# A fused attention and mixer kernel: first query cast shared by two engines, finer pieces of the first keys, earlier pairs of score rounds, and new constants for the static schedule

## The chip, the cores and the metric

The kernel runs on one core of a Trainium2 chip. The metric is the device time of one execution in microseconds (us). An execution counts as fast when it lies within 1.5% of the fastest of its kernel; slow executions are left out of all times and ratios.

## The reference, cut to what matters

```
scores = q @ k^T / sqrt(64) - log(448);  attn = sigmoid(scores);  x = attn @ v
# q, k, v: 8 batches x 12 heads x 448 positions x 64, float32; the heads are put side by side: x is 8 x 448 x 768
h  = relu(x^T @ w_tok1) @ w_tok2          # token mixing, 448 -> 256 -> 448
u  = x + h^T
out = u + relu(u @ w_ch1) @ w_ch2         # channel mixing, 768 -> 1536 -> 768
```

The sigmoid is element by element, so there is no softmax sum to wait for. Heads are handled in quads, three to a batch. A **score round** is four score matmuls, for 64 keys of the four heads of a quad; one sigmoid on ScalarE follows it. (In the very first quad rounds cover half of the heads.)

## The kernel before: the parts that matter here

The program is laid out by a list scheduler in Python that runs before compilation. It keeps an estimated clock for every engine, asks at each step which operations are ready, and takes the one with the best priority. The order it finds is fixed in the program; on the chip the engines only wait for each other. So a changed estimate changes the order of instructions, often far from the place where the estimate was meant to act.

Score rounds have two PSUM slots.

```
for i, hs in both:
    ps = plan.buf("wide", 2, [128, 2, 512], FP32, "psum", f"qk_{b}_{m}_{i}_{hs[0]}")   # two slots
    ...
    nc.tensor.matmul(out=ps[64*s : 64*s+64, h, 0:S], lhsT=kT[...], rhs=qT[...])          # 4 of these
    ...
    nc.scalar.activation(out=at[:, hs, :], in_=ps[:, hs, 0:S], func=SIGMOID, ...)
```

TensorE loses about 0.1 us when it changes between its tiling modes (64-row score and value matmuls, 128-row products); the prediction works this out from the trace. For that reason rounds are grouped in pairs. For batch 1, whose attention is computed beside the mixing of batch 0, the first seven rounds go singly:

```
parts = [[o] for o in rs[:7]] + [rs[i : i + 2] for i in range(7, 21, 2)] + [[o] for o in rs[21:]]
```

The constants REST and REST1 say how much other work (in us of TensorE's time) must be done before the next group of second token products may be taken at its ordinary priority (REST1 is for batch 1; a line left out here gives batch 0's a fixed priority):

```
p = 4.5 if o.name[:2] == "K2" and o.name[-1] == "0" and state["rest"] < (REST1 if o.name[:4] == "K2_1" else REST) else rank
```

The first head's queries come in float32 and are cast by one ScalarE instruction; its transposes on TensorE are cut at position 4, and the second head's keys are kept whole:

```
def cast(raw=raw, h=hs[0]):
    nc.scalar.activation(out=t[:, h, :, :], in_=raw[:, :, :], func=COPYF)
...
whole = [((0, 4), (4, J))]
if lone and hs[0] == 0:
    whole = [((0, 2),), ((2, J),)] if what == "k" else [((0, 4),), ((4, J),)]
```

In the traces, qk is a score matmul, xa a value matmul, c<-uT the first channel product, c<-w_ch the second, kt the first use of the token weights w_tok2, yn and yt second token products, ut a transpose, tq and tk transposes of queries and keys.

## Time and profile before

| kernel before | value | where from |
|---|---|---|
| time | 372.8 us (372.73 to 372.81, 3 runs) | the runs |
| span of the profiled execution | 381.5 us, granted clock 0.949: slow | the cores view |
| span of a second profile of the same kernel | 371.2 us, granted clock 1.0: fast | the cores view |
| TensorE busy in the fast one | 364.5 us of 371.2 (98%) | the page, part 1 |

The prediction had only the slow profile. All comparisons after it use the second, fast profile, which is the first experiment below. "Busy" for TensorE says little here: matmuls overlap and a waiting matmul counts in part. To find lost time I took the start of each matmul, subtracted it from the start of the next, and compared the difference with the streaming time of its columns.

### The profile page before, as it was taken

To read this page: it belongs to the slowest core of one execution; us is meant where nothing else is said; L and a number is where in the kernel's file an instruction comes from. 1 tells how busy PE (TensorE), PEld (TensorE's weight loads), DVE (VectorE), ACT (ScalarE), POOL (GpSimd) and SP (SyncE) were. 2 spreads that over 40 slices of the span, in tenths; PEclk is the share of its full clock that TensorE was granted. 3 is DMA by queue.
4 is the path that set the end of the run, shared out by engine and by line. 5 is a ranking of instruction groups with operands and counts; after the bars stand their busy time and mean duration, and the time that the engine had idled before them with its cause. 6 is when DMAs were issued, how large, how long until landed. Compare 5 with 4: busy or idle time off the path is not lost.

```text
span 381.5 us, 7956 instructions
## 1 busy us (share of the span) xinstructions
PE 374.4 (98%) x3188; PEld 188.2 (49%) x3188; DVE 177.0 (46%) x414; ACT 208.0 (55%) x269; POOL 115.8 (30%) x261
## 2 busy tenths in 40 slices
PE   7999999999999999999999999999999999999995
PEld 4454444554454544455444545544455555555553
DVE  4576345643424545542354335744451358654221
ACT  5997773476677866786667476564556311100000
POOL 8982227144544435334444242350000000000000
PEclk9999999999999999999999999999999999999999
DMA  6999999599989999999998999993004452401344
GB/s 96 185 201 206 210 206 193 107 181 142 142 131 140 196 142 132 124 159 207 166 129 134 182 162 177 184 131 67 18 12 113 101 124 53 63 0 43 82 103 105
DMA packets 97013, 50.06 MB, mean 131 GB/s; under 512 B 70544, under 2 KB 93456, under 8 KB 96976
## 3 DMA queue, kind: packets, MB, share of 16 engines
q0 software_dynamic: 24080, 21.62, 41.7%
q1 hardware_dynamic: 72656, 27.62, 40.2%
q8 instruction: 25, 0.41, 0.4%
q10 hardware_dynamic: 240, 0.31, 0.3%
q14 instruction: 12, 0.10, 0.1%
HBM read 43.45 MB, written 11.01 MB: 143 GB/s over the span
## 4 chain that ended last, share of the span: by engine, by line
PE 94%; POOL 2%; DMA 1%; DVE 1%; ACT 1%; issue 0%; ACTq 0%; POOLq 0%
PE c L1026 30%; PE c L1085 30%; PE qk L595 11%; PE xa L633 9%; PE yn L952 5%; PE k L876 4%; DMA k<-in_k_dram 1%; POOL k L345 1%; PE xb L692 1%; PE k L726 1%; PE k L836 1%; PE k L860 1%; PE tq L540 1%; POOL q L345 1%; PE tk L540 1%; PE yt L910 1%
## 5 line engine op out<-in xcount | busy, mean ns | idle before, releaser
L611 ACT ACTIVATE attn<-qk,att_bias 128x896 f16<-128x896 f32 (+1 forms) x172 | 161.1, 986 | 79.4 <-PE qk L595 76.5
L1026 PE MATMUL c<-uT,w_ch 128*128 128x448 f16 x576 | 122.1, 362 | 0.0
L1085 PE MATMUL c<-w_ch,h2aT 128*128 128x384 f16 x576 | 103.7, 334 | 0.0
L1042 DVE TENSOR_SCALAR h2aT<-c 128x384 f16<-128x384 f32 x96 | 53.5, 557 | 76.6 <-PE c L1026 76.5
L1026 PEld LDWEIGHTS <-w_ch 128*128 128x128 f16 x576 | 54.1, 99 | 60.0 <-issue 12.7
L1085 PEld LDWEIGHTS <-h2aT 128*128 128x128 f16 x576 | 55.7, 100 | 42.6 <-issue 5.8
L1098 DVE TENSOR_TENSOR u<-u,c 128x384 f32<-128x384 f32 x48 | 26.6, 554 | 64.6 <-PE c L1085 64.5
L595 PE MATMUL qk<-qT,kT 64*64 64x448 f16 x672 | 52.6, 366 | 0.6 <-ACT attn L611 0.5
L800 POOL COPY mark<-attn 1x1 f16<-1x1 f16 x54 | 9.6, 178 | 96.6 <-ACT attn L611 96.5
L633 PE MATMUL xa<-attn,v 64*64 64x448 f16 x672 | 37.8, 359 | 0.0
L974 DVE TENSOR_TENSOR u<-x,yn 128x384 f32<-128x384 f16 x48 | 24.7, 550 | 18.0 <-PE yn L952 17.9
L595 PEld LDWEIGHTS <-kT 64*64 64x64 f16 x672 | 14.0, 104 | 31.3 <-issue 29.0
L982 ACT ACTIVATE u<-u 128x768 f16<-128x768 f32 x21 | 17.6, 843 | 19.1 <-DVE u L974 19.1
L670 ACT ACTIVATE xT<-xa 128x448 f16<-128x448 f32 (+2 forms) x61 | 22.1, 439 | 7.5 <-PE xa L633 7.5
L633 PEld LDWEIGHTS <-v 64*64 64x64 f16 x672 | 19.8, 109 | 12.6 <-issue 0.7
L512 POOL COPY qp<-q 128x384 f16<-128x384 f16 (+1 forms) x54 | 21.3, 432 | 11.8 <-DMA q<-in_q_dram 11.0
L512 POOL COPY kp<-k 128x384 f16<-128x384 f16 (+1 forms) x54 | 21.2, 429 | 10.8 <-DMA k<-in_k_dram 10.4
L952 PE MATMUL yn<-h,w_tok 128*128 128x384 f16 x104 | 22.3, 334 | 0.2 <-ACT xT L670 0.2
L1042 DVE TENSOR_SCALAR h2odd<-c 128x64 f16<-128x64 f32 x96 | 20.6, 215 | 0.0
L889 DVE TENSOR_SCALAR h<-k 128x384 f16<-128x384 f32 x24 | 12.8, 557 | 10.2 <-PE k L876 10.2
L1085 PE MATMUL c<-w_ch,h2odd 128*128 128x384 f16 x96 | 17.5, 334 | 0.0
L356 POOL DMA_DIRECT2D q<-in_q_dram x21 | 15.0, 715 | 7.4 <-issue 5.5
(73 smaller groups left out, 208.5 us busy)
## 6 DMA issues: line engine op xcount, KB each, us to landing
out_dram<-u SPq DMA_DIRECT2D x48, 192.0 KB, 2.9
k<-in_k_dram POOLq DMA_DIRECT2D x21, 224.0 KB, 4.7
q<-in_q_dram POOLq DMA_DIRECT2D x21, 224.0 KB, 5.2
v<-in_v_dram POOLq DMA_DIRECT2D x21, 224.0 KB, 5.4
w_ch<-in_moe_w_ch_dram POOLq DMA_DIRECT2D x6, 768.0 KB, 19.1
out_dram<-ut SPq DMA_DIRECT2D x6, 192.0 KB, 3.4
v<-in_v_dram POOLq DMA_DIRECT2D x6, 112.0 KB, 5.2
x<-xT SPq DMA_TRANSPOSE x32, 3.9
```

What stands on the lines that cost most here:

```text
L512: nc.gpsimd.tensor_copy(out=pm[:, to, :, :], in_=src[:, fr, :, :])
L595: nc.tensor.matmul(out=ps[64 * s : 64 * s + 64, h, 0:S], lhsT=kT[64 * h : 64 * h + 64, i, s, :], rhs=qT[64 * h : 64 * h + 64, :, s, :], st ...
L611: nc.scalar.activation(out=at[:, hs, :], in_=ps[:, hs, 0:S], func=SIGMOID, bias=bias_t[:, :], scale=att_scale,)
L633: nc.tensor.matmul(out=ps[s](slice(64 * h, 64 * h + 64)), lhsT=vf[64 * s : 64 * s + 64, h, order[i], :], rhs=attn[i][64 * s : 64 * s + 64, ...
L670: nc.scalar.activation(out=xt[:, s, to : to + n], in_=ps[s](every)[:, fr : fr + n], func=COPYF)
L952: nc.tensor.matmul(out=ps[:, :], lhsT=w_tok2[:, t, s0 : s0 + 2, :], rhs=h1[b][:, t, c], start=(t == 0), stop=(t == 1),)
L974: nc.vector.tensor_tensor(out=to, in0=x, in1=y, op=ADD)
L982: nc.scalar.activation(out=u16[rows, :], in_=utile[rows, :] if blk == 3 else u[b][:, blk, :], func=COPYF)
L1026: nc.tensor.matmul(out=ps[:, :], lhsT=w_ch1[cb // 4][:, db, 128 * (cb % 4) : 128 * (cb % 4) + 128], rhs=uT[b][:, db, :], start=(db == 0), ...
L1042: nc.vector.tensor_scalar(out=to, in0=ps[:, fr], scalar1=0.0, scalar2=None, op0=MAX)
L1085: nc.tensor.matmul(out=ps[:, :], lhsT=h, rhs=w, start=(cb == 0), stop=(cb == NCB - 1))
L1098: nc.vector.tensor_tensor(out=t, in0=t, in1=ps[:, :], op=ADD)
```

## The change

The intent: shorten the first 20 us, in which ScalarE and the loads set the pace, by letting the first score come earlier; then order the stretch where batches 0 and 1 are worked on together so that TensorE has fewer mode changes and waits.

```
-        self.hitch = [(8.6, 1.1), (15.2, 1.4), (19.5, 0.8), (21.9, 0.5)]
+        self.hitch = [(0.1, 0.5), (7.5, 0.3), (8.65, 1.1), (12.4, 0.4), (15.4, 1.0), (19.5, 0.8), (21.9, 0.5)]
...
-    LEAD, SPAN, REST, LATE = 18.0, 0.86, 1.0, 0
+    LEAD, SPAN, REST, LATE = 18.0, 0.86, 1.1, 0
-    JOIN, PULL, ALONE = 0.05, 3.0, 3.5
-    REST1 = 0
-    PAUSE = 1.5
+    JOIN, PULL, ALONE = 0.15, 1.5, 3.5
+    REST1 = 0.1
+    PAUSE = 1.3
...
-                    def cast(raw=raw, h=hs[0]):
-                        nc.scalar.activation(out=t[:, h, :, :], in_=raw[:, :, :], func=COPYF)
+                    for js in (slice(0, 4), slice(4, J)):
+                        eng = "ACT" if not js.start else "DVE"
+                        ...   # ScalarE casts positions 0 to 3, VectorE 4 to 6
...
-            whole = [((0, 4), (4, J))]
+            whole = [((0, 4, 1), (4, J, 1))]
+            if lone and hs[0] and what == "k":
+                whole = [((0, 4, 1),), ((4, J, 1),)]
             if lone and hs[0] == 0:
-                whole = [((0, 2),), ((2, J),)] if what == "k" else [((0, 4),), ((4, J),)]
+                whole = [((0, 2, 1),), ((2, J, 1),)] if what == "k" else [((0, J, 2),), ((1, J, 2),)]
...   # the rest follows from spans having a step; a line that gave the second head's transposes priority is gone
-                parts = [[o] for o in rs[:7]] + [rs[i : i + 2] for i in range(7, 21, 2)] + [[o] for o in rs[21:]]
+                parts = [[o] for o in rs[:5]] + [rs[i : i + 2] for i in range(5, 21, 2)] + [[o] for o in rs[21:]]
```

I call the cast, the transposes and the kept pieces "the start", the last line "the pairs", and REST with REST1 "the rests". "hitch" is a table of expected delays of the loads.

More of the change, by code (lines that the diff above doesn't have):

```diff
@@ L334, in fetch, with cast @@
                             )
-                    def cast(raw=raw, h=hs[0]):
-                        nc.scalar.activation(out=t[:, h, :, :], in_=raw[:, :, :], func=COPYF)
                     o = op("fetch_q", "SQ", 3.0, fetch, uses=[raw])
-                    yield op("cast_q", "ACT", 0.6, cast, [o, warm], [raw, t], rank=-2)
+                    pieces = []
+                    for js in (slice(0, 4), slice(4, J)):
+                        eng = "ACT" if not js.start else "DVE"
+                        def cast(raw=raw, h=hs[0], js=js, eng=eng):
+                            if eng == "ACT":
+                                nc.scalar.activation(out=t[:, h, js, :], in_=raw[:, js, :], func=COPYF)
+                            else:
+                                nc.vector.tensor_copy(out=t[:, h, js, :], in_=raw[:, js, :])
+                        pieces.append(op(f"cast_q{js.start}", eng, 0.09 + 0.075 * (js.stop - js.start), cast, [o, warm], [raw, t], rank=-2))
+                    pieces[0].pieces = pieces
+                    yield pieces[0]
                     continue
@@ L534, in turned, with turn @@
                 parts = []
-                for a, z in spans:
-                    def turn(ps=ps, hs=hs, a=a, z=z):
-                        for i in range(a, z):
+                for a, z, step in spans:
+                    these = range(a, z, step)
+                    def turn(ps=ps, hs=hs, these=these):
+                        for i in these:
                             for h in hs:
@@ L546, in turned @@
                     need = [lds[hs[0]]] if len(lds) > 1 else lds
-                    us = (z - a) * (0.107 if lone and hs[0] == 0 else 0.065)
+                    if step == 2:
+                        need = [need[0].pieces[a]]
+                    us = len(these) * (0.107 if lone and hs[0] == 0 else 0.065)
                     o = op(f"turn{what}_{b}_{m}_{hs[0]}{a}", "PE", us, turn, [*need, ident_op, *hold], [raw, ps, ident, t])
                     o.pri = (0 if what == "q" else 0.05) + (0.35 if m == 2 else 0) if b == 0 else 2.5
-                    if lone and hs[0] and a:
-                        o.pri = -1.5
                     parts.append(o)
@@ L557, in turned @@
                 extra.extend(parts)
-                eng = "ACT" if spans[0] in ((0, 2), (4, J)) else "DVE"
-                pieces = [(eng, slice(spans[0][0], spans[-1][1]))]
+                eng = "ACT" if spans[0] in ((0, 2, 1), (1, J, 2)) else "DVE"
+                pieces = [(eng, slice(spans[0][0], spans[-1][1], spans[0][2]))]
                 for eng, ij in pieces:
@@ L568, in turned @@
                     o = op(
-                        f"keep{what}_{b}_{m}_{hs[0]}{ij.start}", eng, 0.08 + 0.08 * (ij.stop - ij.start), keep, parts, [t, ps], rank=-1 if b == 0 else 0.5
+                        f"keep{what}_{b}_{m}_{hs[0]}{ij.start}", eng, 0.08 + 0.08 * len(range(J)[ij]), keep, parts, [t, ps], rank=-1 if b == 0 else 0.5
                     )
```

## The prediction

> **What bounds the kernel now.** I read the page first, for the busiest engine and for the chain that ended last.
>
> ```profile
> PE 374.4 (98%) x3188; PEld 188.2 (49%) x3188; DVE 177.0 (46%) x414; ACT 208.0 (55%) x269; POOL 115.8 (30%) x261
> ...
> PE 94%; POOL 2%; DMA 1%; DVE 1%; ACT 1%; issue 0%; ACTq 0%; POOLq 0%
> ```
>
> TensorE is busy 98% of the span and carries 94% of the chain; what is not TensorE (POOL, DMA, DVE, ACT, together 5%, some 19 us) lies almost wholly in the first 20 us. The change alters no large piece of TensorE's work, so it can pay only where TensorE waits or changes mode. The profiled execution was a slow one (381.5 us span, granted clock 0.949, against 372.8 us timed). I use it for durations and waits, and apply savings in us to 372.8: waits at the start are mostly other engines' time.
>
> To find TensorE's lost time I compared each matmul's start to the next one's start with its streaming time. In steady runs a 448-column matmul takes 0.197 us from start to start. The chain in order of time shows it, and the price of a mode change:
>
> ```profile
> 36.49 0.68 PE c L1026 x3
> 37.48 0.69 PE c L1026 x3
> 38.49 1.87 PE c L1026 x9
> ```
>
> (1.87 - 0.68) / 6 = 0.198 us a matmul. Between 36.49 and 37.48 there stand three of these (0.59 us) and one score round of 64-row matmuls (one more stream, 0.197 us): 0.99 - 0.79 = 0.20 us is left, two mode changes, about **0.1 us each**. By that account TensorE loses per 2 us about 1.2 us until 10, 0.6 to 0.8 us from 12 to 20, and from 20 us on almost nothing but mode changes, except at two places: near 64 us (0.46 us) and at 105.7 us (0.6 us). So there are three things to look at: the first 20 us, the two bubbles, the count of mode changes.
>
> The timeline shows the start (start, duration, engine, what, idle before and releaser):
>
> ```profile
> 3.79 0.58 ACT L337 ACTIVATE q<-q_first 128x448 f16<-128x448 f32 x1 [0.92 <-DMA q_first<-in_q_dram]
> ...
> 6.14 0.57 PE L595 MATMUL qk<-qT,kT 64*64 64x448 f16 x4
> ...
> 6.56 1.16 ACT L611 ACTIVATE attn<-qk,att_bias 128x448 f16<-128x448 f32 x2 [0.82 <-PE qk L595]
> ...
> 7.96 6.33 ACT L611 ACTIVATE attn<-qk,att_bias 128x448 f16<-128x448 f32 x9 [0.25 <-PE qk L595]
> ...
> 13.79 0.41 PE L540 MATMUL tk<-ident,k 128*64 128x128 f16 x8 [0.16 <-DMA k<-in_k_dram]
> ...
> 14.57 1.01 ACT L611 ACTIVATE attn<-qk,att_bias 128x896 f16<-128x896 f32 x1 [0.28 <-PE qk L595]
> ...
> 15.73 10.76 ACT L611 ACTIVATE attn<-qk,att_bias 128x896 f16<-128x896 f32 x11 [0.15 <-PE qk L595]
> ...
> 16.12 1.16 DVE L664 CAST xT<-xa 128x448 f16<-128x448 f32 x2 [0.64 <-PE xa L633]
> ...
> 21.07 0.95 PE L760 MATMUL kt<-w_tok,h 128*128 128x448 f16 x4
> ...
> 64.64 0.93 PE L952 MATMUL yn<-h,w_tok 128*128 128x384 f16 x4 [0.20 <-ACT xT L670]
> ```
>
> The reader is to see that from 6.56 us the sigmoids on ScalarE nearly touch, with idle times of 0.25, 0.28 and 0.15 us: ScalarE bounds the start, and the 0.28 arises because the score matmul stands behind a transposition that waits for keys landing at 13.65 us. From 16.12 to 20.5 us VectorE works without a break too.
>
> **What the Trainium skill says.** "ScalarE: Activation LUTs", What ACT_TABLE_LOAD costs: an activation with immediate scale and bias takes 186 ns + 0.833 ns per element of the row. For 448 elements that is 559 ns; the trace has 576, so it agrees. "TensorEngine Tiling (Array Packing)", Key Properties: changing the tiling mode drains TensorE; the trace agrees, at 0.1 us a change. "SBUF — State Buffer", SBUF: two separate sides: a VectorE fp32 copy from SBUF to SBUF can take the port pair that GpSimd needs to write DMA descriptors. The kernel before has no such copy, so no run yet shows it; it is a rival below.
>
> **The change, part by part.** The instruction orders of the two programs give the rest.
>
> (a) **The first cast in two.** ScalarE's part falls to 128x256: 0.186 + 0.213 = 0.40 us (estimate by the page), ending near 4.19 instead of 4.37. VectorE's 128x192 is an estimate of 0.25 to 0.35 us, from its copies of 512 and 896 columns (0.417 and 0.627 us, slope 0.55 ns, intercept 0.14 us), ending near 4.1, while VectorE is otherwise idle. Query transposes then go first (odd positions, then even, 0.055 us each, from about 4.25); keys of head 0 landed at 4.46, all seven follow and end near 5.05. ScalarE copies the odd queries (0.48 us, to 5.07), then two keys (0.38 us, to 5.4). The first score matmul no longer stands behind the second head's query transposes, which waited for a landing at 5.75 and start at 5.88 in the timeline. I expect it at 5.43 instead of 6.14, the first sigmoid at 5.85 instead of 6.56: **0.7 us earlier**.
>
> (b) **Second-head keys in two parts.** The third score matmul waits only for a PSUM slot: near 6.5 instead of 7.55. The fourth waits behind four key transposes for the landing at 6.93, so an idle time of some 0.3 us opens at that sigmoid. The first round of head 1 needs just four key columns (0.42 us on VectorE instead of 0.63). Its sigmoid is at 8.4 instead of 9.06: 0.7 us ahead.
>
> (c) **New constants for the expected landings.** Score round 0 of quad 1 now stands ahead of the key transposes that waited until 13.79, but behind value matmuls that need values landed at 12.12: from 12.25, twenty take 1.0 us, so it comes at 13.35 and its sigmoid at 13.75 instead of 14.57. Over the 20 us ScalarE gains 0.7 + 0.25 + 0.28 + 0.15 and loses about 0.6 in new idle times: **0.8 us ahead** at 15 us. Not all of it reaches the end. VectorE follows at 15.3 instead of 16.12, but its w_tok spreads need a load that landed at 18.18 whatever the change. From 18.3 (18.44 in the timeline before): two spreads 0.8, the third (moved ahead) 0.65, two relus 0.8: 20.5, as before. TensorE's first matmul on w_tok2 had 0.5 us of slack behind that (it started at 21.07 because of TensorE's own order), so it comes at about 20.65: **-0.4 us**. From there TensorE is dense in both programs, so this shift lasts to the end.
>
> (d) **Batch 1's rounds in twos from the sixth.** Between the first channel work and its second product there are 20 mode changes instead of 22: **-0.2 us**.
>
> (e) **REST, JOIN, PULL, PAUSE** spread batch 0's and 1's token products among other work. Before, a product at 64.64 waited for a PSUM bank that ScalarE had to empty (0.46 us lost). After, channel products stand there, and VectorE, at 0.55 us an add, has freed the banks: **-0.45 us**. In return the last transpose of batch 1's u stands just before its first channel product with one pair of rounds between: copy 0.45 plus 0.26 us hand-over against 0.65 us of work, **+0.1 us**, and two more mode changes there, **+0.2 us**. Around batches 5 and 6 the odd-row products now ride with score rounds: 4 changes fewer, **-0.4 us**. The bubble at 105.7 us stands in the same order and stays.
>
> Sum: -0.4 - 0.2 - 0.45 + 0.1 + 0.2 - 0.4 = -1.15 us. Three fillers more stand in waiting time and cost nothing. A reordered schedule tends to open one wait that I don't see, so I take -1.0: **371.8 us**.
>
> **The rivals.** First: the loads bound the start, and the gain of (a) to (c) is taken back by waits for landings or by VectorE. For it: landings from 8.5 to 19 us come 0.5 to 0.6 us apart, VectorE is full from 16 to 20.5. Against: TensorE's slack ahead of 21.07. It would leave -0.75 us, 372.05. Second: VectorE's new cast holds up GpSimd's descriptors (its issues at 4.01 and 4.51), all later landings slip by up to 0.3 us, and the start gains nothing or loses: 372.2 to 372.6. Third: the whole 0.8 us passes through, if the w_tok2 load lands earlier than in this slow execution: 371.4. Fourth: new bubbles between 60 and 90 us, where transposes by DMA of batch 1's u now come after a store in the queue: up to +1 us, 372.8.
>
> **Range and chances.** The steps span 371.4 (all pass) to 372.8 (all taken back); I widen the lower end for work I undervalued: 371.1 to 372.6. A gain of 2% would be 7.5 us, as much as half of all that TensorE loses in the first 20 us and more than the change touches; a loss of 2% would need several new stalls in a program whose work is the same. Faster 0.01, same 0.985, slower 0.005.
>
> **What would show it.** In the changed profile: first sigmoid near 5.85 (a); the head-1 sigmoids from 8.4 (b); quad 1's first sigmoid near 13.75 and the first w_tok2 product at 20.5 to 20.8 (c); no wait on ScalarE's xT near 64 us (e); fewer mode changes from 60 us on and, through fillers, more in the idle start (221 in all against 217). I am wrong if the first w_tok2 product is not earlier than 21.0, if a wait above 0.3 us stands between 60 and 90 us, or if GpSimd's issues near 4 us take longer than 0.55 us. All times in a slow execution shift a little with its clock.

## The result, and the profile after

The changed kernel took **371.25 us** (median of 6 runs, 370.94 to 371.54) against 372.81 us (6 runs, 372.39 to 373.68) in the same rounds. Ratios are computed as the mean time of one kernel's fast runs over that of the other's fast runs of the same rounds, so they are not quite the ratio of the medians quoted. Here the ratio is 0.9954, with a 95% interval from 0.9942 to 0.9967: 1.7 us less than 372.8, and well inside "within 2%". The direction and the class were as predicted; the gain was 1.7 us where 1.0 was predicted. Taken from 372.8 this gives 371.09 us, just under the low end of the range (371.1); the plain median, 371.25, lies just inside it.

The page of the changed kernel (busy time by engine; then the chain that ended last, by engine), from a fast execution with a span of 369.7 us:

```profile
PE 364.2 (99%) x3191; PEld 186.6 (50%) x3191; DVE 177.3 (48%) x416; ACT 207.8 (56%) x269; POOL 115.5 (31%) x261
...
PE 97%; DVE 1%; ACT 1%; issue 0%; DVEq 0%
```

TensorE's busy time is what it was in the fast profile of the kernel before (364.5 us). The span got shorter by 1.5 us because TensorE waits less.

The timeline of its start (start, duration, engine, what, count; in brackets the idle time before and what ended it; "..." stands for lines left out):

```profile
3.70 0.42 ACT L343 ACTIVATE q<-q_first 128x256 f16<-128x256 f32 x1 [0.84 <-DMA q_first<-in_q_dram]
3.70 0.26 DVE L345 CAST q<-q_first 128x192 f16<-128x192 f32 x1
...
4.06 2.24 POOL L354 DMA_DIRECT2D k<-in_k_dram  x4
...
6.17 0.86 PE L607 MATMUL qk<-qT,kT 64*64 64x448 f16 x4
...
6.79 1.16 ACT L623 ACTIVATE attn<-qk,att_bias 128x448 f16<-128x448 f32 x2 [0.68 <-PE qk L607]
...
21.02 0.93 PE L772 MATMUL kt<-w_tok,h 128*128 128x448 f16 x4
```

The two casts run side by side, 0.42 and 0.26 us. The first score round and the first sigmoid are hardly earlier (6.17 and 6.79 us) than in the fast profile of the kernel before (6.30 and 6.85), although the prediction said 5.43 and 5.85. The reason is TensorE's clock, shown in the experiments.

The view of waits for TensorE (what waited for what: us in total, times, longest), first of the changed kernel, then of the kernel before in its fast profile, where "..." stands for waits of the first 22 us:

```profile
PE idle L488 <- DVE att_bias L292: 1.2, 1, 1.2
PE qk L607 <- ACT attn L623: 0.2, 1, 0.2
```

```profile
...
PE qk L595 <- ACT attn L611: 0.3, 1, 0.3
PE yn L952 <- ACT xT L670: 0.2, 1, 0.2
...
```

The two waits shown of the kernel before are the two bubbles that the prediction spoke of, near 64 us (the token product yn) and near 105 us (the score round qk). Both are gone. The first, near 64 us, was expected to go; the second was expected to stay. The first in the trace of the kernel before (by the starts of its matmuls it costs 0.37 us, and 0.11 us more at the next step):

```profile
64.03 0.92 PE L952 MATMUL yn<-h,w_tok 128*128 128x384 f16 x4 [0.21 <-ACT xT L670]
```

The second in the same trace (TensorE and ScalarE):

```profile
99.80 2.44 PE L1026 MATMUL c<-uT,w_ch 128*128 128x448 f16 x12
102.17 0.57 PE L595 MATMUL qk<-qT,kT 64*64 64x448 f16 x8
102.67 3.70 ACT L611 ACTIVATE attn<-qk,att_bias 128x896 f16<-128x896 f32 x4 [1.03 <-PE qk L595]
102.67 1.31 PE L1026 MATMUL c<-uT,w_ch 128*128 128x448 f16 x6
103.91 0.38 PE L595 MATMUL qk<-qT,kT 64*64 64x448 f16 x4
104.62 0.38 PE L595 MATMUL qk<-qT,kT 64*64 64x448 f16 x4 [0.33 <-ACT attn L611]
```

and the same place in the changed kernel:

```profile
100.11 0.57 PE L607 MATMUL qk<-qT,kT 64*64 64x448 f16 x8
100.61 1.91 ACT L623 ACTIVATE attn<-qk,att_bias 128x896 f16<-128x896 f32 x2 [1.03 <-PE qk L607]
100.62 2.44 PE L1038 MATMUL c<-uT,w_ch 128*128 128x448 f16 x12
102.99 0.57 PE L607 MATMUL qk<-qT,kT 64*64 64x448 f16 x8
```

A pair of rounds is 8 qk matmuls. ScalarE needs 1.91 us for the two sigmoids of a pair. In the kernel before, only six channel matmuls (1.31 us) stand between the pair at 102.17 and the next. When the next pair begins at 103.91, one of the two PSUM slots is free and the other still belongs to a sigmoid. So the pair is torn: its second round starts 0.71 us after the first. The streaming time of a round is 0.57 - 0.38 = 0.19 us (in the whole pair at 100.11, the second round starts 0.21 us after the first), so TensorE loses 0.71 - 0.19 = **0.52 us**. (The bracket says 0.33, because ends of matmuls are modelled; starts are the safer measure.) In the changed kernel twelve matmuls (2.44 us) stand there and the pair is whole.

### The profile page after: what moved, and what is told of

It is laid out like the page before. It is cut to its first block, busy times and chain, and to the rows that moved or that the text cites. A ratio compares the mean times of both kernels' runs of the same rounds, so it can differ in the third digit from the quotient of the medians.

```text
span 369.7 us, 7967 instructions
## 1 busy us (share of the span) xinstructions
PE 364.2 (99%) x3191; PEld 186.6 (50%) x3191; DVE 177.3 (48%) x416; ACT 207.8 (56%) x269; POOL 115.5 (31%) x261
## 4 chain that ended last, share of the span: by engine, by line
PE 97%; DVE 1%; ACT 1%; issue 0%; DVEq 0%
PE c L1097 30%; PE c L1038 30%; PE qk L607 12%; PE xa L645 9%; PE yn L964 5%; PE k L888 4%; PE tk L552 1%; PE tq L552 1%; PE xb L704 1%; PE k L738 1%; PE idle L488 1%; PE k L848 1%; PE k L872 1%; PE yt L922 1%; PE fill L503 1%; ACT attn L623 1%
## 5 line engine op out<-in xcount | busy, mean ns | idle before, releaser
L1038 PE MATMUL c<-uT,w_ch 128*128 128x448 f16 x576 | 117.8, 353 | 0.1
L1097 PE MATMUL c<-w_ch,h2aT 128*128 128x384 f16 x576 | 100.0, 326 | 0.0
L645 PE MATMUL xa<-attn,v 64*64 64x448 f16 x672 | 36.3, 349 | 0.0
```

Of the source, the lines that this page charges most:

```text
L645: nc.tensor.matmul(out=ps[s](slice(64 * h, 64 * h + 64)), lhsT=vf[64 * s : 64 * s + 64, h, order[i], :], rhs=attn[i][64 * s : 64 * s + 64, ...
L1038: nc.tensor.matmul(out=ps[:, :], lhsT=w_ch1[cb // 4][:, db, 128 * (cb % 4) : 128 * (cb % 4) + 128], rhs=uT[b][:, db, :], start=(db == 0), ...
L1097: nc.tensor.matmul(out=ps[:, :], lhsT=h, rhs=w, start=(cb == 0), stop=(cb == NCB - 1))
```

## The experiments

My theory after reading the two traces: the gain has two sources, the start and the stretch from 60 to 105 us; in the latter a torn pair is repaired, because the schedule puts more than ScalarE's 1.9 us between pairs. The rivals: the gain is all from the start; or a single constant does it; or the cast on VectorE is what matters.

All outputs are right. The kernel before ran in the same rounds each time. In the middle of this section a table splits every profile at TensorE's first product with w_tok2 (kt), because from there on TensorE is dense.

### b_again: the kernel before, once more

No edit; it serves to get a profile of a fast execution, and to show how far a kernel differs from itself.

> The kernel before, unchanged, as a null test and to get a profile of it at full clock. Ratio 1.000 within 0.002. All theories: the two bubbles near 64 us and 105 us (0.46 and 0.6 us in the slow profile) are there again at about 62 and 102 us; if the one near 105 us is absent at full clock, it can't be part of the gain. The time at which TensorE's clock is let go (4.2 us in one trace, 6.8 us in the other) should differ from execution to execution if it is chance.

372.93 us (372.4 to 373.56), ratio 1.001 [0.9997, 1.0022], with a span of 371.2 us at clock 1.0. So a tenth of a per cent can come from nothing, which is 0.4 us.

### start_only: the start alone

The first part of the diff (cast, transposes, kept pieces), with the constants, the hitch table and the pairs of the kernel before.

> Only the structure of the start is changed: first cast in two, query positions odd and even, keys of head 1 in two parts; old constants, old rounds of batch 1. Theory of the prediction: -0.4 us (ratio 0.999). Rival (the start gave more, 0.8 us or all of the 1.6): ratio 0.9978 or 0.9957. The schedule further on is shuffled as a side effect, so the trace is to be read by stages: first w_tok2 matmul at 20.6 or earlier against 21.0.

374.69 us (374.05 to 375.62), ratio **1.0059** [1.0045, 1.0073]: slower. Yet its start did what was wanted: kt begins at 20.39 us instead of 21.45. The loss comes later. Other estimates at the start led the scheduler to another order further on, with new waits such as these (timeline of TensorE):

```profile
135.37 1.29 PE L1038 MATMUL c<-uT,w_ch 128*128 128x448 f16 x6 [0.65 <-DVE uT L1016]
...
164.51 1.15 PE L1097 MATMUL c<-w_ch,h2aT 128*128 128x384 f16 x6 [0.88 <-DVE ut L954]
```

The start is a gain only together with an order that does not give it back. The hitch table is not what is missing here: built with the changed kernel's table, and with its JOIN, PULL and PAUSE, start_only has the same order on TensorE from kt on. (That is a build, not a run.)

### pairs_only: batch 1's rounds in twos from the sixth

```
-parts = [[o] for o in rs[:7]] + [rs[i : i + 2] for i in range(7, 21, 2)] + ...
+parts = [[o] for o in rs[:5]] + [rs[i : i + 2] for i in range(5, 21, 2)] + ...
```

> Only batch 1's rounds in twos from the sixth. Two mode changes fewer before the second product of the channel part: prediction -0.2 us (ratio 0.9995). Rival (the pairs shift everything so that the bubble near 64 us or the one near 105 us goes): -0.6 to -1.0 us (ratio 0.998 or less).

372.86 us (372.37 to 373.6), ratio 1.0006 [0.9993, 1.0018]: nothing. The trace shows that this nothing is a sum. The wait near 64 us is gone and two mode changes with it; the torn pair near 104 us is still there, and a second torn pair has appeared at 83.02 us, again behind only six matmuls.

### mid_only: pairs and all constants but the hitch table, with the old start

```
-    LEAD, SPAN, REST, LATE = 18.0, 0.86, 1.0, 0
+    LEAD, SPAN, REST, LATE = 18.0, 0.86, 1.1, 0
-    JOIN, PULL, ALONE = 0.05, 3.0, 3.5      REST1 = 0      PAUSE = 1.5
+    JOIN, PULL, ALONE = 0.15, 1.5, 3.5      REST1 = 0.1    PAUSE = 1.3
     and the line of pairs_only
```

> All constants of the middle (REST, REST1, JOIN, PULL, PAUSE) and the pairs, with the start as before. If the middle carries the gain beyond the start: -0.2 (pairs) -0.45 (bubble at 64) = -0.65 us, ratio 0.9983; with the bubble at 105 gone as well -1.2 us, ratio 0.997. If the start carries it: ratio 0.9995.

371.52 us (371.33 to 372.65), ratio **0.9975** [0.9963, 0.9988]: 0.9 us less than before. Of the waits named so far none is left in its trace.

JOIN, PULL and PAUSE need no run. The changed kernel built with their three old values has the same order of instructions on every engine as with the new ones, and mid_only too. What is left of the constants is the rests. Of these REST does nothing either: with its old value alone the order of the changed kernel, and of mid_only, stays the same, and with the old REST1 alone it is that of after_no_rests below. So "the rests" is in effect the one constant REST1.

### after_no_rests: the changed kernel with the old REST and REST1

```
-    REST = 1.1, REST1 = 0.1
+    REST = 1.0, REST1 = 0
```

> The changed kernel with REST and REST1 as before (30 lines of TensorE's order, all between 65 and 100 us). Batch 1's first channel matmuls stand directly behind the value matmuls again, so the bubble near 104 us should come back: +0.65 us against the changed kernel, ratio 0.9972; the bubble near 64 us stays away, for the pairs removed that. Rival (the pairs removed both): 0.9955.

372.13 us (371.98 to 372.3), ratio 0.9973 [0.9961, 0.9985]. The torn pairs of pairs_only are back, at 82.99 and 104.04 us. The first in its timeline:

```profile
81.04 1.15 PE L1097 MATMUL c<-w_ch,h2aT 128*128 128x384 f16 x6
82.12 0.38 PE L607 MATMUL qk<-qT,kT 64*64 64x448 f16 x4
82.99 0.38 PE L607 MATMUL qk<-qT,kT 64*64 64x448 f16 x4 [0.49 <-ACT attn L623]
```

Six matmuls of 384 columns are 1.15 us, still shorter than six of 448, and the tear is wider: 0.87 - 0.19 = 0.68 us. In the changed kernel second token products, transposes and twelve channel matmuls stand between the pair at 78.91 and the one at 82.13 us, and twelve channel matmuls between the pairs at 100.11 and 102.99 us.

### late_c1 and late_c1yn: repairing the torn pair of the kernel before by force

late_c1 makes the first channel work of batch 1 wait for one more score round, so that it lies differently against the pairs; late_c1yn moves a token product too, to remove the wait near 64 us.

```
-    for late, first_ in ():
+    for late, first_ in (("C1_1_0", "S_2_1_4"),):                               # late_c1
+    for late, first_ in (("C1_1_0", "S_2_1_4"), ("K2_0_2_1", "C2_0_0_1")):      # late_c1yn
```

> The kernel before with one line more: batch 1's first channel matmul may start only after the next pair of score rounds. Nothing else moves (10 lines of TensorE's order, none on the other engines): every channel piece of batch 1 stands one place later against the score pairs, so 12 matmuls instead of 6 stand ahead of the last pair near 104 us. My theory (the step that failed in the prediction is the bubble near 105 us, which the change takes away by this shift): the 0.65 us bubble is gone and two mode changes with it, -0.65 - 0.2 = -0.85 us, ratio 0.9977. Rival (the bubble is no loss, the time comes back later): ratio 1.000.

> The line of late_c1 and one more: batch 0's token product that waited for a PSUM bank near 64 us stands behind the next channel product (17 lines of TensorE's order in all). Both bubbles gone: -0.85 - 0.45 = -1.3 us, ratio 0.9965, with the start as before. If that holds, two lines in the middle give most of what the change gave; if the change's gain is of the start, this gives clearly less than the change.

late_c1: 373.07 us (372.9 to 375.54), ratio 1.0014 [0.9991, 1.0038]. late_c1yn: 373.12 us (372.61 to 374.88), ratio 1.0006 [0.9987, 1.0026]. Neither gained anything. In late_c1 the torn pair at 104 us is gone, but another stands at 85.8 us. Its timeline, with ScalarE:

```profile
83.40 0.57 PE L595 MATMUL qk<-qT,kT 64*64 64x448 f16 x8
83.80 1.49 PE L633 MATMUL xa<-attn,v 64*64 64x448 f16 x28
83.83 1.90 ACT L611 ACTIVATE attn<-qk,att_bias 128x896 f16<-128x896 f32 x2 [0.59 <-PE qk L595]
85.13 0.36 PE L595 MATMUL qk<-qT,kT 64*64 64x448 f16 x4
85.79 0.38 PE L595 MATMUL qk<-qT,kT 64*64 64x448 f16 x4 [0.31 <-ACT attn L611]
```

Now a group of value products, 1.49 us, is the only work between two pairs, and that is too little as well. The experiment fails as a remedy and helps as a measurement. Take the gap from the start of the work behind a pair to the start of the next pair: gaps of 1.08 us (after_no_rests, 81.04 to 82.12), 1.24 (before, 102.67 to 103.91) and 1.33 (here, 83.80 to 85.13) tear a pair and cost 0.68, 0.52 and 0.66 - 0.19 = 0.47 us. Gaps of 1.87 us (changed kernel, a value group and six transposes from 82.53 to a pair at 84.40) and 2.37 us (100.62 to 102.99) do not. The profile of start_only has one between: a gap of 1.65 us, from 224.74 to 226.39, costs 0.15 us. I went through every case behind kt in which one pair follows another, in all fast profiles: each gap of 1.65 us or less tears its pair, and none of 1.86 us or more does. That the bound lies somewhat below 1.9 us is to be expected, since the second round comes 0.21 us behind the first anyway; from the torn pair of the kernel before it is estimated at 104.62 - 0.21 - 102.67 = 1.74 us. In late_c1yn the wait near 64 us did not go either: the next token product took the moved one's place and lost the same 0.37 us.

### cast_act: both parts of the first cast on ScalarE

```
-    nc.vector.tensor_copy(out=t[:, h, js, :], in_=raw[:, js, :])
+    nc.scalar.activation(out=t[:, h, js, :], in_=raw[:, js, :], func=COPYF)
```

> The changed kernel with the second part of the first cast issued on ScalarE too (all orders else the same). Theory (the start's gain is capped by VectorE and the w_tok2 load, so the cast is worth little at the end): first score matmul 0.2 to 0.35 us later, first w_tok2 matmul at most 0.1 us later, time within 0.1 us of the changed kernel (ratio 0.9955 +- 0.001). Rival (the cast is on the path): +0.3 us, ratio 0.9963.

371.15 us (370.7 to 372.21), ratio 0.9953 [0.9936, 0.9969], the same as the changed kernel's 0.9954. The engine of the second part makes no difference that these runs can show. GpSimd's issue of the four key loads from 4.0 us on took 2.25 us here and 2.24 us in the changed kernel, but the VectorE cast (3.70 to 3.96 us) is over by then. What runs beside it is the second issue of a query load, from 3.50 us. It took 0.52 us here and in the kernel before. Of the six profiles that have the cast, it took 0.52 us in four, but 0.57 and 0.58 us in the changed kernel and in fix_ride; and in two of the four, after_no_pairs and fix_hold, the cast itself took 0.32 and 0.38 us instead of 0.26. So the two seem to get in each other's way at times, by 0.05 to 0.12 us; no run tests this, and at kt it doesn't show above the scatter.

### after_no_pairs and rests_only: the missing corners

The pattern so far suggested that pairs and rests act on separate waits. These two runs test it: the changed kernel with the old pairs, and the kernel before with the rests alone.

```
-parts = [[o] for o in rs[:5]] + [rs[i : i + 2] for i in range(5, 21, 2)] + ...     # after_no_pairs
+parts = [[o] for o in rs[:7]] + [rs[i : i + 2] for i in range(7, 21, 2)] + ...
```

```
-    REST = 1.0, REST1 = 0          # rests_only
+    REST = 1.1, REST1 = 0.1
```

> The changed kernel with batch 1's rounds in twos only from the eighth round on, as in the kernel before; all else as in the changed kernel. My theory: the wait of 0.4 to 0.5 us near 64 us (a token product behind a PSUM bank that ScalarE empties) was removed by the pairs and not by the new constants, so it comes back, with 0.2 us of mode changes, while the wait at 104 us stays away, for it was removed by the constants REST and REST1: a ratio of about 0.997 to 0.998. The prediction on record said the contrary: the constants remove the wait near 64 us; then it stays away here and only 0.2 us are lost: 0.996.

> The kernel before with the two constants REST = 1.1 and REST1 = 0.1 alone. My theory: they put twelve instead of six channel matmuls between the two pairs of score rounds near 100 to 104 us, so the wait of 0.65 us there goes, the wait near 64 us stays, unless the later token products move it; a ratio of 0.998 to 0.9985 (0.5 to 0.7 us less than before). The rival: the constants work only together with the pairs (alone they move just 16 groups of TensorE's order, together with them 30), then the wait at 104 us stands as before and the ratio is 1.000.

after_no_pairs: 372.75 us (371.87 to 373.51), ratio 0.9988 [0.9967, 1.0009]. rests_only: 372.92 us (372.92 to 374.01), ratio 1.0000 [0.9978, 1.0022]. My theory of separate waits was wrong, in both runs. The wait near 64 us came back without the pairs, as I expected, but the torn pair near 104 us did as well. From after_no_pairs:

```profile
63.52 0.92 PE L964 MATMUL yn<-h,w_tok 128*128 128x384 f16 x4 [0.21 <-ACT xT L682]
...
103.41 0.38 PE L607 MATMUL qk<-qT,kT 64*64 64x448 f16 x4
104.11 0.38 PE L607 MATMUL qk<-qT,kT 64*64 64x448 f16 x4 [0.33 <-ACT attn L623]
```

In rests_only too both stand unchanged (64.60 and 105.19 us). So the rests do not remove the torn pair alone. Pairs bring one pair more into the stretch before batch 1's channel work; the rests hold back enough other work to give this pair its distance. Only both together shift the channel work of batch 1 by one pair: in the traces with both it begins with 15 matmuls behind a pair, in those of the kernel before, of pairs_only, of rests_only and of the two corners of the changed kernel it begins with six matmuls ahead of a pair.

### The table: from the first w_tok2 product to the end

The start of kt and the span are from each trace; the last column is their difference.

| version | start | pairs | rests | kt at | span | kt to end |
|---|---|---|---|---|---|---|
| b_again | old | old | old | 21.45 | 371.16 | 349.71 |
| pairs_only | old | new | old | 20.93 | 370.60 | 349.67 |
| rests_only | old | old | new | 22.02 | 371.92 | 349.90 |
| mid_only | old | new | new | 21.08 | 369.74 | **348.66** |
| start_only | new | old | old | 20.39 | 372.28 | 351.89 |
| after_no_rests | new | new | old | 20.67 | 370.34 | 349.67 |
| after_no_pairs | new | old | new | 20.72 | 370.42 | 349.70 |
| after | new | new | new | 21.02 | 369.66 | **348.64** |

This is the main result. (Each row is one profile. cast_act, whose order is that of the changed kernel, has 348.82 us in the last column, so 0.2 us is scatter. start_only has the old hitch table too.) Behind kt, pairs alone give 0.04 us, rests alone nothing, both together **1.05 us** with the old start and 1.07 with the whole change. With pairs or rests in place the start gives nothing behind kt; alone it costs 2.2 us there, which either of the other two takes back. What the start gives must be in kt's own column.

That column scatters. The six profiles with the old start (with late_c1 at 21.47 and late_c1yn at 22.21) have kt at 20.93 to 22.21 us, mean 21.53. The seven with the new start (with cast_act at 20.41 and the two runs below at 21.95 and 21.31) have 20.39 to 21.95 us, mean 20.92. The means differ by 0.6 us, but the ranges overlap. Nor is it the order: up to kt this is one and the same on TensorE in b_again, pairs_only, rests_only and mid_only, and one and the same in the changed kernel, after_no_pairs, after_no_rests, cast_act and the two below. Two causes of the scatter show in the traces. One is the third load of queries: in fix_hold below, a transpose waited 1.4 us for its landing, until 16.85 us; in the changed kernel the same transpose began at 15.91 without a wait. The other is TensorE's clock. Seven transposes of the first queries, in the changed kernel and in after_no_rests, whose first 20 us are built alike:

```profile
4.53 0.95 PE L552 MATMUL tq<-ident,q 128*64 128x128 f16 x7
```

```profile
4.22 0.58 PE L552 MATMUL tq<-ident,q 128*64 128x128 f16 x7
```

The first ran at half speed, 0.107 us from start to start, the second at 0.055 us. Full speed was reached at about 6.8 us in the one and 3.85 us in the other, and 6.6 us in b_again (estimates from the spacing of the matmuls that straddle it). So the profiles of before and after happen both to be late ones, which makes them comparable with each other, and neither shows the start at its best. In after_no_rests the first score matmul comes at 5.42 us and the first sigmoid at 5.84.

### fix_hold and fix_ride: is there a better version?

The changed kernel has one wait of its own behind 20 us: 0.29 us at 231.6 us. A token product of batch 5's odd rows rides with a pair of score rounds, its PSUM is emptied by four VectorE adds of 0.55 us each, and only then VectorE can free the bank for the channel matmuls. Two constraints that move one of the two:

```
-    for late, first_ in ():
+    for late, first_ in (("C1_4_0", "K2_5_0_1"),):     # fix_hold: channel work behind the token product
+    for late, first_ in (("V2_5", "C1_4_2"),):         # fix_ride: the product rides with a later pair
```

> The changed kernel with one constraint more: the first channel work of batch 4 stands behind the second token product of batch 5's odd rows, so that the token products near 231 us, one of which waits 0.29 us for a bank that VectorE frees late in the changed kernel, stand elsewhere. If that wait goes and no other opens: 0.25 to 0.3 us less than the changed kernel, a ratio of about 0.9945 against 0.9953. If another wait takes its place: 0.995 to 0.997.

> The changed kernel with another constraint for the same wait near 231 us: a group of value products of batch 5 stands behind the third channel round of batch 4, which gives the odd rows' token product another pair of score rounds to ride with; the count of mode changes is the same (221). If the wait of 0.29 us goes and no other opens: a ratio of about 0.9945. If another wait takes its place: 0.995 to 0.997.

fix_hold: 372.75 us (372.38 to 374.17), ratio 0.9995 [0.9974, 1.0017]; it is the worse for its constraint. The wait grew, since the channel matmuls now come right behind the token product and wait for all four adds:

```profile
232.64 1.31 PE L1038 MATMUL c<-uT,w_ch 128*128 128x448 f16 x6 [1.75 <-DVE ut L954]
```

fix_ride: 371.08 us (371.06 to 371.66), ratio 0.9950 [0.9930, 0.9971]. The wait moved from 231.6 to 242.6 us, where it measures 0.35 us; kt to the end takes 348.57 us against 348.64. The median is the lowest of all versions by 0.07 us, which these intervals cannot tell from cast_act or from the changed kernel. I don't count it as a better version. It does support the reading of the wait: it goes wherever the odd rows' product goes.

## Why the prediction was right or wrong, point by point

**What bounds the kernel: right.** TensorE's lost time decides. In the kernel before there were, from kt on, exactly the two larger losses that the prediction named (0.48 us in two steps near 64 us, 0.52 us near 104 us), and the rest was mode changes, but for 0.1 us near 233 us.

**(a) and (b), the first scores: right in mechanism, with the clock in the way.** In the profiles whose clock came early (after_no_rests, start_only, cast_act, fix_ride) the first score matmul is at 5.42 to 5.54 us (predicted 5.43) and the first sigmoid at 5.84 to 5.96 (5.85); with the old start and an early clock (pairs_only, rests_only, late_c1, late_c1yn) they are at 6.08 to 6.28 and 6.50 to 6.70. Where the clock came late the gain is small: the first sigmoid is at 6.58 us in after_no_pairs and 6.79 in the changed kernel, against 6.85 in b_again. The second head's first sigmoid, the fifth in order, is at 8.59 to 8.63 us with an early clock, where 8.4 was predicted, against 8.84 to 9.21 in those four with the old start: 0.2 to 0.6 us ahead, not 0.7. The gain comes from the order on TensorE: the first score no longer stands behind the second head's query transposes. The shared cast itself, which gives the change its name, is worth nothing measurable (cast_act).

**(c), 0.4 us at the first w_tok2 product: the path was right, the size is open.** In after_no_rests, with its early clock, the path can be followed: quad 1's first sigmoid is at 13.69 us (predicted 13.75; 14.53 in pairs_only), the second relu on VectorE ends at 20.43 (predicted 20.5) and kt begins at 20.67 (predicted 20.65). This is one profile, the one whose clock came earliest; in the changed kernel's own the relu ends at 20.48, but TensorE has other work and begins kt at 21.02. b_again to after gives 0.44 us; the means of all profiles 0.6; the time ratios, taken with and without the start at equal pairs and rests, 0.5 us (after_no_pairs against rests_only: 0.9988 and 1.0000), 0.8 us (after against mid_only: 0.9954 and 0.9975) and 1.2 us (after_no_rests against pairs_only: 0.9973 and 1.0006). With intervals of 0.4 us and more to each side of each ratio, 0.4 to 1.2 us is all that can be said.

**(d), two mode changes fewer by the pairs: the count is right, the value is not.** By itself the part gave nothing, because it tears a pair at 83 us (0.68 us) while it removes the wait at 64 us.

**(e), the step that failed.** Three larger things were wrong in it. The first is the term that the sum lacked: "The bubble at 105.7 us stands in the same order and stays." It does not stand in the same order. The order of the changed kernel has twelve channel matmuls instead of six between the two pairs, and the bubble is gone: **0.52 us** that I counted as zero. I had compared the order at the pair itself, not the work ahead of it. The second is whose merit it is. I gave the end of the wait near 64 us to REST, JOIN, PULL and PAUSE; it goes with the pairs (pairs_only has it no longer, after_no_pairs has it again), and these four constants do nothing to the order at all. REST1, which does, I had not named. The third is the late part: I expected four mode changes fewer around batches 5 and 6 by odd rows that ride with score rounds, 0.4 us. From kt to the end there are 184 mode changes instead of 186 (counted in the traces). My terms gave four fewer (two, less two, and four): two more between kt and the first channel work, which I had missed, take half of that back. And the riding has a price that I had not seen, the wait of 0.29 us at 231.6 us. And the 0.1 us that I had set down against the change, for the last transpose of batch 1's u, did not appear: the channel product behind it, at 84.92 us, follows its pair without a wait.

**The sum.** From kt on: 0.48 + 0.52 us of waits gone, 0.2 us of mode changes gone, and 0.17 us more near 231 to 234 us (0.29 in the changed kernel, 0.12 in the kernel before), makes 1.03 us; the profiles show 1.07. My terms behind kt made 0.75 us. With the 0.6 us that the means of the profiles give for the start this is 1.7 us, which is what was measured; as the start's worth is open between 0.4 and 1.2 us, the agreement proves little. The allowance of 0.15 us for a wait that I didn't see was of the right kind and size, but the sum to which it was applied was too small.

**The rivals.** The first (loads and VectorE take the start back) is not supported as a rule, though one late landing can do it in a single execution, as in the profile of fix_hold, which has the new start and kt at 21.95 us. The second (GpSimd held up) may show, with 0.05 us in two profiles; the 0.3 us that it feared does not. The third (0.8 us pass whole) can't be told from the 0.4 to 1.2 above. The fourth (new bubbles from 60 to 90 us) is what pairs_only and after_no_rests have, and the changed kernel escapes by the rests.

**My own signs of being wrong.** The first w_tok2 product was to come before 21.0 us; in the profile of the changed kernel it comes at 21.02. By the letter the sign fired; four of the other six profiles of the new start have 20.39 to 20.72. No wait above 0.3 us stands between 60 and 90 us in the changed kernel. GpSimd's first two issues behind 4 us took 0.52 and 0.54 us, within the 0.55 allowed; the one beside the cast, at 3.50 us, took 0.57.

What stays open: the exact worth of the start, and why start_only's order a hundred us later becomes so much worse. The traces show its waits; which estimate of the new start led the scheduler there was not traced; the hitch table it was not.

## What to carry to other kernels

When an engine fills a buffer of two slots in pairs, the work between pairs should last about as long as the consumer needs for a pair, here 1.9 us of sigmoids: a gap of 1.65 us still cost something, 1.87 us nothing. Count that work in the order of the instructions, gap by gap; it is as plain there as in a trace. Parts of a change that only alter a schedule can be worth nothing singly and something together, so test them in a full table of on and off, and read beside the time which waits went and which came. And a short start profiled once says little: the same kernel's first 20 us differed by a us from run to run.

## What the Trainium skill lacked or had wrong

- "TensorEngine Tiling (Array Packing)", Key Properties, says that a change of tiling mode drains TensorE and gives no cost. Here it is about 0.1 us a change, and the kernels make 184 to 186 of them behind the first 21 us, an estimate of 18 us in all.
- "TensorE: Matmul & The Clock Gate", Part 1, says that the release of the clock varies from run to run, at 107 ns against 56 ns for a matmul of 128 columns. The runs agree (0.107 and 0.055 us). But the page puts the release at around 4 us of matmuls, within half a us from run to run, and here it came by the estimates above 2.7 to 5.6 us after the first matmul at 1.17 us. The page also calls the clock events in a trace unreliable; here is a case of such a figure: the granted clock read 1.00 in every stretch from 2 to 20 us that I asked for in b_again, in the changed kernel and in after_no_rests, although in the first two TensorE ran at half speed until about 6.6 and 6.8 us.
- "SBUF — State Buffer", SBUF: two separate sides, led me to the rival in which a VectorE cast holds up GpSimd's descriptors. It gives no size for a cast as short as this one (128x192 from float32 to float16, 0.26 us). Here the issue beside it took at most 0.05 us longer: 0.57 and 0.58 us in two profiles of six, 0.52 us in the others and without the cast.
- No page that I used puts a figure to the spacing of score rounds against sigmoids with two PSUM slots. Here gaps between pairs of 1.08, 1.24 and 1.33 us cost 0.68, 0.52 and 0.47 us, and gaps of 1.87 and 2.37 us nothing, with 1.9 us of ScalarE's time for a pair.
